# A fused cross-attention and mixture-of-experts kernel: the first batch loaded as fp32 through hardware DMA queues, GpSimd given subtractions, and a new written-out instruction order

## Chip, cores, metric

The kernel runs on one core of a Trainium2 chip. The metric is device time in microseconds, median of several executions. A core has five engines with a queue each, which run their instructions in order: TensorE (PE, with weight loads shown as PEld), VectorE (DVE), ScalarE (ACT), GpSimd (POOL) and SyncE (SP). SP and ACT issue DMAs through hardware queues, POOL through a software queue, which can also convert fp32 to fp16 on the way. Engines wait for one another through semaphores.

## What is computed

The reference, cut to its core (B, H, S, D = 8, 8, 512, 64, with 32 state rows for each head; the second part has 4352 rows of 512, 8 experts, hidden size 1024):

```python
scores = scale * x @ state.T                 # per batch and head
a = softmax(scores, -1);  xread = a @ state  # 512 rows
scores2 = scale * state @ x.T
a2 = softmax(scores2, -1); sread = a2 @ x    # 32 rows
x = concat([xread, sread], 2) -> (B*544, 512)
logits = x @ w_gate; P = exp(logits - max)
for _ in range(8):                           # Sinkhorn: rows, then columns
    P /= P.sum(1) + 1e-9; P /= P.sum(0) + 1e-9; P *= N / E
for e in range(E):
    out += P[:, e:e+1] * (relu(x @ w1[e]) @ w2[e])
```

## The kernel before

All matrix products run in fp16 with fp32 sums. The work has two parts.

**Part one, up to about 134 us, is an order written out by hand.** Every step is an `Op` with the engines that it may run on, and with the steps and buffers it waits for. They are numbered as they are made. `PLAN` is a table of steps, such as `56P`: number 56, on PE (V is DVE, A ACT, G POOL, S the SP queue, H nothing on the device). `issue` walks through `PLAN` and emits one step after the other, so the table sets both the engine of a step and its place in that engine's queue. The figures beside the engines, such as `(0.44, 0.62)`, and attributes such as `since` and `goal` were used by whatever drew the table; they have no effect on the device.

The steps of part one, with their lines:

- *State.* `state` is loaded as fp32 by two DMAs (L441, on SP and ACT, four batches each, in rows of 256 bytes), cast into `st_in` twice side by side (`place`), transposed on PE (L492) and copied into `stT`. `stD`, a block-diagonal form, serves the first two score blocks.
- *x.* Each batch of x is loaded in two halves of four heads, fp32 converted to fp16 by POOL's queue (L468). For batches 0 and 1 PE transposes it (L578) and DVE or ACT copies it out as `xT`; for the others a DMA transpose from SP does (L591).
- *Score blocks S0 to S15,* two for each batch. PE computes scores into one pair of PSUM banks (L605); a second form for the first two blocks is L684. The A side (softmax over the state): DVE transposes (`flip`, L628), maximum (L631), subtraction (`subA`, L648), exp on ACT (L656), sum and reciprocal on DVE (L666, L667), product on DVE or POOL (`normA`, L670), transpose back into `aT` (L674, or PE and a copy for the first two). The B side (softmax over the tokens): maximum (L640), exp on ACT (L652), reciprocal (L659), product (`normB`, L662), DMA transpose of `E2` into `ETs` (L742), and PE's read of x (L758).
- *Expert 0.* V = state times w1 (L870, two halves for each batch), hidden layer hps = V times aT (L897), second layer yps (L935).
- *Gate and Sinkhorn* (L788, L814 to L846), w2 sums of expert 1 for the second part (`sums_w`, L965, eight subtractions on DVE), and the first hidden block of expert 1.

**Part two, from about 134 us, is ordinary loops** over experts 1 to 7 and 9 row blocks: `layer1` (L255 on PE, relu L275 on ACT, sums L281 to L284 on DVE), `layer2` (seven half-size products L334 where there would be eight, added into `acc` by L348), `project` (L235) and `load_w`.

PE is in order, so a step that waits holds all that stands behind it in `PLAN`. The same holds for POOL's queue, in which loads of x and weights stand between its products.

Of the kernel before, what the change touches and what calls it, by code (L numbers as in the profile page):

```python
# [16 lines left out]
6G 0S 1S 2V 7H 44V 3A 33V 32A 34A 8G 56P 36P 35V 55H 37V 10H 45V 57A 42P 58V 9G 38P 40P 43A 59P 4S 39A 41V 5V  # L17
46V 62P 50H 51G 61A 71V 63P 60A 52G 64V 11G 72V 73A 80P 65V 12G 435P 401P 66A 81V 13H 79P 14G 82V 436A 88V
437A 404P 83A 67V 402A 137H 403A 89V 96H 97P 100P 84V 406A 68V 90A 98A 15G 85V 69P 86P 53G 405A 99V 87V 70A
103P 101A 102A 91V 409P 16H 92G 413P 104V 407P 410A 411P 105V 111A 438P 120P 414V 408A 419P 421P 106V 415P  # L20
112V 138S 121V 74V 439A 412A 422V 113V 417P 107A 54G 440A 75G 122V 432P 429P 123V 370V 420A 469P 128A 418A
416A 17G 108V 140P 124A 125V 423P 426P 471A 433P 114A 148V 93S 129V 430P 149V 172H 424P 76S 434A 115V 470A
109G 130V 139S 110V 126G 141V 131A 427P 18G 127V 142V 428V 431A 445P 143V 132V 94P 150A 95V 77P 425A 156P 116G
447P 151V 133V 78V 449P 446A 443P 441P 144A 455P 164V 152G 448A 117S 19H 450V 157V 444A 165V 173S 442A 451P
456A 166A 134S 20G 452A 453P 463P 158V 472P 207H 145V 175P 159V 183V 184V 457P 31G 146G 454A 176V 473A 160A
464P 185A 174S 460P 458P 461P 465A 147V 161V 21G 153S 177V 191P 47P 162G 474A 118P 167V 459A 154P 462A 178V
163V 135P 49A 168G 199V 22H 48V 179A 466P 136A 352P 475P 200V 192V 201A 193V 119V 467P 476A 194V 23G 195A 485P
202V 208S 210P 180V 169S 155A 218V 356P 353A 481P 357V 468A 487P 219V 24G 489P 181G 186V 211V 242H 486A 482A
477P 490V 488A 483P 479P 220A 170P 478A 503P 187G 480A 484V 171A 203G 196V 537P 209S 25H 212V 226P 197G 504A
505A 506P 213V 500P 182V 198V 26G 234V 221V 507A 222V 204S 188S 491P 27G 538A 227V 539A 501P 497P 502A 508A  # L30
492P 235V 243S 228V 244S 214A 229V 511P 215V 236A 523P 230A 498P 494P 216G 245P 495P 515P 512V 499A 277H 231V
524A 493A 517P 246V 253V 223S 496A 247V 521P 516A 237V 254V 519P 509P 522V 518A 248V 513P 232G 189P 520A 255A
205P 510V 224P 514V 540P 28H 278S 261P 249A 190V 269V 29G 225A 270V 262V 531P 534P 206V 238G 250V 532P 256V
358P 271A 535P 217V 541A 533A 233V 542A 312H 279S 263V 272V 536A 354P 280P 528P 543P 529P 525P 288V 289V 251G
555P 264V 281V 265A 282V 239S 257V 526P 359A 266V 544A 530V 556A 545P 355A 547P 549P 273G 553P 527A 546V 571P
313S 290A 548A 283V 605P 550A 554V 296P 267G 606V 304V 572A 305V 240P 573A 557P 284A 607A 558A 551P 297V 552A
568P 360P 258S 241V 285V 30G 291V 306A 559P 562P 574P 298V 252V 315P 299V 286V 569P 576A 268V 323V 563P 575A
274S 300A 560P 570A 292G 316V 361A 561A 581P 564A 307V 565P 362P 324V 317V 301V 325A 302G 566P 363V 582A 326V
579P 587P 583P 287V 314S 588V 591P 567A 580A 639P 608P 584A 592A 347H 303V 331P 577P 348G 641V 640A 610A 609A
339V 293S 589P 585P 275P 332V 259P 578A 327G 586A 260A 590A 294P 340V 308G 333V 341A 593P 309S 318V 319A 334V  # L40
295V 364P 594P 276V 328S 625P 619P 342V 595A 335A 365A 599P 320V 602P 343V 336V 600P 337V 603P 626A 321G 322V
329P 310P 350G 344S 601A 349G 311A 620V 345P 338V 346V 604V 366P 596P 330A 368P 369V 351G 597P 367A 371V 611P
372P 598A 695H 615P 617P 373V 612V 374P 375V 613P 614V 616A 623P 618A 621P 696H 711H 376A 705P 377V 642P 624A
622A 706A 707A 630P 643V 697V 708P 644A 378P 379V 631P 710A 627P 698V 380V 647P 632A 709A 636P 628P 381P 633P
699V 648V 637P 382V 634P 657P 629A 638A 383V 700V 653P 658A 655P 384P 651P 635A 701V 654A 725P 385V 723P 386V
702V 656A 726A 716P 652A 724A 717A 645P 659P 649P 714P 646A 650A 660A 387P 721P 715A 712P 727P 687P 722A 388V
728A 688A 667P 713A 664P 389V 390P 703V 665P 668P 391V 673P 674A 392V 661P 670P 669A 729V 393P 671P 394V 666A
662P 672A 677P 395V 718P 663A 678A 679P 675P 683P 719A 681P 720V 680A 676A 685P 396P 684A 682A 397V 686A 692P
704V 689P 693P 690P 730P 398V 694A 399P 733P 731V 691A 732A 735A 734A 400V
# [55 lines left out]
def issue(ops):  # L105
    for step in PLAN:
        op = ops[int(step[:-1])]
        assert all(d.end for d in op.after) and ENGINES[step[-1]] in op.on
        for slot in op.takes:
            slot.ring.taken.append(slot)  # L110
            slot.tile = slot.make()
        op.emit(ENGINES[step[-1]])
        op.end = True
    assert all(op.end for op in ops) and len(PLAN) == len(ops)
# [3 lines left out]
def kernel(  # L118
# [99 lines left out]
    etp = actx.enter_context(tc.tile_pool(name="attn_et", bufs=3))  # L218
# [216 lines left out]
    st_in = spl.tile([128, B, NQ, 2, D], FP16, name="st_in")  # L435
    st_st = spl.tile([128, B, NQ, D], FP32, name="st_st")
    loads = []
    for g in range(2):
        def load(g=g):
            bs = ds(g * B // 2, B // 2)  # L440
# [3 lines left out]
        loads.append(dma((0, 0), 1.0, load, lands=2.7))  # L444
        ops[-1].since, ops[-1].hard = 0.5, 1
# [5 lines left out]
    wgd = dma((0, 2), 0.1, lambda: nc.sync.dma_start(  # L451
        out=wg_st, in_=moe_w_gate.rearrange("(kc p) e -> p kc e", p=128)))
    wgc = op((15.0,), {"DVE": (0.15, 0.25)}, lambda _: nc.vector.tensor_copy(out=wgh, in_=wg_st), [wgd])
    wgc.since = 20.0
# [7 lines left out]
    for b in range(B):  # L462
        x_ready.append([])
        part("x%d" % b)
        got = op((0, 1 + 2 * b), {"HOST": (0.0, 0.0)}, lambda _: None, takes=[xn[b]])
        for g in range(2):
            def load(b=b, g=g):
# [4 lines left out]
            x_ready[b].append(dma((0, 1 + 2 * b, g), 1.28 if b else 2.3 - 0.6 * g, load, [got], [], [xn[b]], "POOL"))  # L472
            ops[-1].since, ops[-1].hard = 0.7, 1
# [4 lines left out]
    bd = []  # L478
    for g in range(2):
        for s_ in range(2):  # L480
            def place(eng, g=g, s_=s_):
                bs = ds(g * B // 2, B // 2)
                copy(eng, st_in[:, bs, :, s_, :], st_st[:, bs])

            bd.append(op((0, 0, g), {"DVE": (0.50, 0.64)} if s_ else {"ACT": (0.50, 0.65)}, place, loads[g:g + 1] + warmed))
    stT_ready = []
    for g in range(4):
        ps = psum([128, 4, 128], FP16, "stT_ps")

        def turn(_, g=g, ps=ps):  # L490
            for i in range(4):
                nc.tensor.transpose(ps.tile[:, i], st_in[:, 2 * g + i // 2, i % 2].rearrange("p s d -> p (s d)"),  # L492
                                    identh)

        def keep(eng, g=g, ps=ps):
            copy(eng, stT[:, ds(2 * g, 2)].rearrange("p b q c -> p (b q) c"), ps.tile)

        t = op((0, 1, g), {"PE": (0.35, 0.55)}, turn, bd[g // 2 * 2:g // 2 * 2 + 2] + [makeh], [ps])
        stT_ready.append(op((0, 1, g), EVICT16, keep, [t], uses=[ps]))
    ND = (TOK + 1) // 2  # L500
    stD_ready = {}
    if TOK:
        stD = spl.tile([128, ND, NQ, 4, 2, Ns], FP16, name="stD")
        zd = op((0, 0, 0), {"POOL": (0.40, 0.50), "DVE": (0.25, 0.35)}, lambda eng: engines[eng].memset(stD, 0.0))
        for b in range(ND):
            def spread(eng, s_, b=b):
# [4 lines left out]
                               lambda eng, s_=s_, spread=spread: spread(eng, s_), stT_ready[b // 2:b // 2 + 1] + [zd])  # L511
# [55 lines left out]
    for b in range(B):  # L567
# [4 lines left out]
                  [x_ready[b][0]], [xT])  # L572
        for g in range(2 if b < NT else 0):
# [11 lines left out]
            t = op((due_x(2 * b + g) - 2.0, 0), {"PE": (0.70, 0.88)}, turnX, [x_ready[b][g], makeh], [ps], [xn[b]])  # L585
# [3 lines left out]
        for g in range(0 if b < NT else 2):  # L589
# [5 lines left out]
            xt_ready.append([dma((due_x(2 * b - 2), 0, g), 2.0, turn, [x_ready[b][g], gotT], [], [xn[b], xT], lands=0.8)])  # L595
            ops[-1].moves, ops[-1].xbar = (3.0, 0.8), 1
            ops[-1].on = {"SPQ": (1.4, 4.5)}
        for q in range(NQ):
# [18 lines left out]
            o2 = op((due_x(2 * b + q), 0), {"PE": (0.13, 0.38)}, score, xt_ready[q] + stT_ready,  # L617
# [5 lines left out]
            E2 = slot(etp, 3, [128, S], FP16, "E2")  # L623
            a16 = slot(asb, 2, [128, S // 32, Ns], FP16, "a16")
            ETs = slot(etp, 3, [128, NSC, 128], FP16, "ETs")
# [402 lines left out]
    n = 0  # L1028
# [79 lines left out]
```

## Time and profile before

| | |
|---|---|
| median of 3 runs | 754.13 us (753.98 to 754.52) |
| the profiled execution | 753.05 us, of which the profile's span is 751.3 us |
| mean granted TensorE clock | 0.997 |
| PE / DVE / ACT / POOL busy | 98% / 82% / 69% / 9% |
| DMA | 36.71 MB in 51,323 packets |
| first PE instruction | 6.98 us |
| first hidden-layer matmul of expert 0 (L897) | 18.66 us |
| first layer-2 matmul of expert 1 (L334) | 134.45 us |

Busy time is a union of an engine's instructions; PE's are pipelined, so what counts for PE is also how far apart its matmuls start (0.216 us for 128x512 at full clock). Instructions on DVE and ACT overlap a little too: 128x512 in fp32 lasts 0.68 us on DVE, and the next one starts 0.60 us after it. A wait is put down to what released it last. The granted clock is the share of full speed that PE was allowed.

### The profile page before, as it was taken

Reading aid. Unit: us, or ns where it says so; the run is one execution under the profiler, and the core shown is the slowest. Engines: PE = TensorE matmul, PEld = TensorE weight load, DVE = VectorE, ACT = ScalarE, POOL = GpSimd, SP = SyncE. Lnnn points to the kernel's source line nnn. Section 1 sums busy time; section 2 is a strip of 40 time slices with the busy share of each in tenths; the row PEclk is TensorE's granted clock in tenths of the full one; section 3 lists DMA queues with packets and bytes.
Section 4 is the critical chain, followed back from the end, with each engine's and each line's share of the span. In section 5 each row is a group of like instructions: output and inputs, shape, how many; then the busy total and the mean of one; then the engine's idle time right before and its main releaser. Section 6 shows DMA issues by size and latency. Waiting matters only on the chain.

```text
span 751.3 us, 16144 instructions
## 1 busy us (share of the span) xinstructions
PE 734.7 (98%) x6517; PEld 501.2 (67%) x6517; DVE 616.3 (82%) x1529; ACT 518.2 (69%) x1014; POOL 70.8 (9%) x81
## 2 busy tenths in 40 slices
PE   4999999999999999999999999999999999999997
PEld 3444445667677777777777677776777777776776
DVE  5999989888888789788887888887897888878875
ACT  6876846798976766666666766667667666676662
POOL 3664310200010000100000000100001000000000
PEclk9999999999999999999999999999999999999999
DMA  9997560600032000600006000330006000002234
GB/s 175 151 133 127 86 92 1 113 2 1 1 66 48 2 1 2 113 1 1 2 4 110 2 1 1 58 56 1 1 2 112 2 1 2 1 29 101 98 113 141
DMA packets 51323, 36.71 MB, mean 49 GB/s; under 512 B 25392, under 2 KB 43824, under 8 KB 51248
## 3 DMA queue, kind: packets, MB, share of 16 engines
q0 software_dynamic: 22272, 20.97, 18.4%
q1 hardware_dynamic: 27744, 14.18, 7.7%
q8 instruction: 51, 0.84, 0.5%
q10 hardware_dynamic: 1232, 0.52, 0.3%
q14 instruction: 24, 0.20, 0.1%
HBM read 42.48 MB, written 8.91 MB: 68 GB/s over the span
## 4 chain that ended last, share of the span: by engine, by line
PE 91%; DVE 3%; DMA 2%; ACT 1%; POOL 1%; issue 0%; SPq 0%; POOLq 0%; ACTq 0%
PE hps L255 28%; PE Bseed L334 20%; PE A L334 14%; PE E L334 13%; PE yps L935 6%; PE v_ps L235 4%; PE hps L897 4%; DMA xT<-x_nat 2%; DMA x_nat<-in_x_dram 1%; DVE acc L348 1%; ACT Hm L275 1%; PE su_ps L758 0%; PE y L312 0%; PE v_ps L870 0%; POOL E L662 0%; ACT V L419 0%
## 5 line engine op out<-in xcount | busy, mean ns | idle before, releaser
L275 ACT ACTIVATE Hm<-hps 128x512 f16<-128x512 f32 (+1 forms) x496 | 265.2, 577 | 128.1 <-PE hps L255 125.3
L255 PE MATMUL hps<-aT,V 128*128 128x512 f16 x880 | 230.1, 379 | 0.0
L334 PEld LDWEIGHTS <-Hm 128*128 128x128 f16 x1888 | 181.4, 98 | 71.2 <-issue 15.8
L348 DVE SCALAR_TENSOR_TENSOR acc<-Bseed,Pmat,acc 128x256 f32<-128x256 f32 x354 | 155.0, 477 | 9.4 <-PE Bseed L334 6.6
L334 PEld LDWEIGHTS <-sm 128*128 128x128 f16 x1416 | 138.2, 98 | 34.1 <-issue 0.4
L334 PE MATMUL A<-w2h,Hm 128*128 128x256 f16 x944 | 123.7, 273 | 0.0
L334 PE MATMUL Bseed<-T,Hm 128*128 128x256 f16 x944 | 123.3, 273 | 0.0
L255 PEld LDWEIGHTS <-V 128*128 128x128 f16 x880 | 86.1, 98 | 51.3
L348 DVE SCALAR_TENSOR_TENSOR acc<-E,Pmat,acc 128x256 f32<-128x256 f32 x236 | 103.1, 476 | 12.5 <-PE E L334 12.5
L281 DVE TENSOR_TENSOR sm<-Hm 128x512 f16<-128x512 f16 (+1 forms) x122 | 50.1, 411 | 64.2 <-ACT Hm L275 64.0
L243 ACT CAST V<-v_ps 128x512 f16<-128x512 f32 x150 | 77.7, 611 | 0.0
L348 DVE SCALAR_TENSOR_TENSOR acc<-A,Pmat,acc 128x256 f32<-128x256 f32 x118 | 51.9, 479 | 17.2 <-PE A L334 16.7
L935 PE MATMUL yps<-w2h,hT 128*128 128x512 f16 x272 | 64.1, 379 | 0.0
L363 ACT COPY Bseed<-A 128x512 f32<-128x512 f32 (+1 forms) x62 | 34.1, 550 | 43.3 <-PE A L334 42.1
L334 PE MATMUL E<-T,sm 128*128 128x256 f16 x472 | 61.7, 273 | 0.0
L334 PE MATMUL E<-w2h,sm 128*128 128x256 f16 x472 | 61.7, 273 | 0.0
L334 PE MATMUL Bseed<-T,sm 128*128 128x256 f16 x472 | 61.5, 272 | 0.0
L282 DVE TENSOR_TENSOR Hm<-Hm 128x512 f16<-128x512 f16 (+1 forms) x122 | 50.2, 412 | 4.2
L284 DVE TENSOR_TENSOR sm<-Hm,sm 128x512 f16<-128x512 f16 (+1 forms) x122 | 50.2, 412 | 4.2
L283 DVE TENSOR_TENSOR sm<-sm,Hm 128x512 f16<-128x512 f16 (+1 forms) x122 | 49.4, 405 | 0.0
L194 POOL DMA_DIRECT2D w1h<-in_moe_w_dram x12 | 8.5, 714 | 397.9 <-PE hps L255 397.4
L935 PEld LDWEIGHTS <-hT 128*128 128x128 f16 x272 | 25.4, 99 | 28.8 <-issue 1.7
(127 smaller groups left out, 609.7 us busy)
## 6 DMA issues: line engine op xcount, KB each, us to landing
w1h<-in_moe_w_dram POOLq DMA_DIRECT2D x16, 512.0 KB, 7.0
w2h<-in_moe_w_dram POOLq DMA_DIRECT2D x16, 512.0 KB, 8.1
out_dram<-acc SPq DMA_DIRECT2D x32, 256.0 KB, 2.6
x_nat<-in_x_dram POOLq DMA_DIRECT2D x16, 256.0 KB, 5.6
st_st<-in_state_dram ACTq DMA_DIRECT2D x1, 256.0 KB, 4.9
st_st<-in_state_dram SPq DMA_DIRECT2D x1, 256.0 KB, 4.3
ETs<-E SPq DMA_TRANSPOSE x16, 3.9
out_dram<-acc SPq DMA_DIRECT2D x4, 64.0 KB, 1.7
```

Of the source, the lines that this page charges most:

```text
L235: nc.tensor.matmul(ps[q][ds(j * Ns, Ns), :], stT[ds(r, 64), bi, q, ds((j ^ q) * Ns, Ns)], w1h[ds(r, 64), 2 * q + j // 2, cols], tile_posit ...
L243: nc.scalar.copy(out=dst, in_=src)
L255: nc.tensor.matmul(out, lhs, rhs, start=(k == 0), stop=(k == len(terms) - 1))
L275: nc.scalar.activation(out=Hm[:, i, j, :tn], in_=hps[:, :tn], func=AF.Relu)
L281: nc.vector.tensor_add(s1, a21, a22)
L282: nc.vector.tensor_sub(a21, a11, a21)
L283: nc.vector.tensor_sub(s2, s1, a11)
L284: nc.vector.tensor_sub(s4, a12, s2)
L334: nc.tensor.matmul(dst[:, c], lhs(j, c), rhs[:, j], start=first and c == 0 and j == 0, stop=(j == NJ - 1), skip_group_check=True)
L348: nc.vector.scalar_tensor_tensor(out=dst, in0=src[:, c], scalar=p[:, k], in1=dst, op0=ALU.mult, op1=ALU.add)
L363: nc.scalar.copy(out=Bb[:, :nk], in_=A[:, :nk])
L935: nc.tensor.matmul(yps.tile, hT[fb].tile[:, ds(tk * 128, 128)], w2h[:, fb, :], start=(fb == 0), stop=(fb == NFB - 1))
```

## The change

- `PLAN` is another table: nearly all of part one stands in another order. The instructions of part two are the same.
- Batch 0 of x is loaded as raw fp32 by four DMAs of two heads each, two on SP and two on ACT, into rows of `acc` that are not in use yet, and cast to fp16 by DVE and ACT (`narrow`). Batches 1 to 7 go through POOL's queue as before.
- State is laid out in rows of 1 KB and in four groups of two batches. Group 0 is loaded ahead of x0 on SP; group 1 follows behind x0 on SP, groups 2 and 3 go first through POOL's queue. The steps of a batch wait for its own group (`st_ready(b)`), not for all.
- `IDLE` puts 79 dummy matmuls or transposes of the identity in front of eight PE steps of the opening. They write a PSUM tile that the step then overwrites.
- Of 14 `subA`, 11 run on POOL (none before); of the 8 `sums_w`, 5 do. `normB` on POOL is a product of two tensors where it was one with a scalar per row (11 on POOL, 12 before); `normA` has 13 on POOL, 12 before. The memset of `stD` moves to POOL.
- Both copies of `aT` for batch 0 run on DVE (one was on ACT). `E2` and `ETs` have four buffers each, three before. w_gate is loaded once the first state group is in place.
- PE's queue holds 13,166 instructions (13,008 before); the 158 more are the dummies, two each.

```diff
+IDLE = {38: 33, 63: 12, 69: 2, 87: 5, 442: 9, 107: 12, 93: 4, 44: 2}
+XH = 2
+NE2 = 4
...
-    etp = actx.enter_context(tc.tile_pool(name="attn_et", bufs=3))
+    etp = actx.enter_context(tc.tile_pool(name="attn_et", bufs=NE2))
...
-            (nc.scalar if g else nc.sync).dma_start(
-                out=st_st[:, bs], in_=state[bs].rearrange("b (q h) n d -> (h n) b q d", q=NQ))
+    st_rows = state.rearrange("b h (k l) d -> (b h k) (l d)", l=4).rearrange("(g p) c -> p g c", p=128)
+    xs = acc[:, ds(0, 2 * XH), :].rearrange("p (g t) d -> p g (t d)", t=2)
+    def load_st(a, b):
+        return begin("SPQ", lambda: nc.sync.dma_start(out=st_st[:, a:b], in_=st_rows[:, a:b]), 0.35 * (b - a))
+    def load_x(g, k):
+        q = nc.scalar if k else nc.sync
+        return begin("ACT" if k else "SPQ", lambda: q.dma_start(
+            out=xs[:, g, ds(k * 512, 512)].rearrange("p (h c) -> p h c", h=2),
+            in_=x[0, ds(4 * g + 2 * k, 2)].rearrange("h (p sc) d -> p h (sc d)", sc=NSC)), 0.68)
+    loads = load_st(0, 1)
+    xs_in = [[load_x(g, k) for k in range(2)] for g in range(XH)]
+    for a, b in ((1, 2), (2, B // 2)):
+        def load_rest(eng, a=a, b=b):
+            (nc.gpsimd if eng == "POOL" else nc.sync).dma_start(out=st_st[:, a:b], in_=st_rows[:, a:b])
...
+            if not b and g < XH:
+                def narrow(eng, g=g, k=0):
+                    copy(eng, xn[0].tile[:, ds(4 * g + 2 * k, 2), :].rearrange("p h c -> p (h c)"),
+                         xs[:, g, ds(k * 512, 512)])
...
-        t = op((0, 1, g), {"PE": (0.35, 0.55)}, turn, bd[g // 2 * 2:g // 2 * 2 + 2] + [makeh], [ps])
+        t = op((0, 0, g), {"DVE": (0.55, 0.64), "ACT": (0.62, 0.72)}, place, [loads[g]] + warmed)
+        t = op((0, 1, g), {"PE": (0.35, 0.55)}, turn, [t, makeh], [ps])
+    st_ready = lambda b: [stT_ready[b // 2]]
+    wgd = dma((0, 2), 0.1, lambda: nc.sync.dma_start(
+        out=wg_st, in_=moe_w_gate.rearrange("(kc p) e -> p kc e", p=128)), [stT_ready[0]])
...
             def normB(eng, E2=E2, rrec=rrec):
-                engines[eng].tensor_scalar(out=E2.tile, in0=E2.tile, scalar1=rrec.tile, scalar2=None,
-                                           op0=ALU.mult)
+                if eng == "POOL":
+                    nc.gpsimd.tensor_mul(E2.tile, E2.tile, rrec.tile.broadcast_to((128, S)))
+                else:
+                    nc.vector.tensor_scalar(out=E2.tile, in0=E2.tile, scalar1=rrec.tile, scalar2=None, op0=ALU.mult)
...
-                s1 = op(r(4), {"DVE": (0.60, 0.80)}, subA, [m1], [], [eA, mxA])
+                s1 = op(r(4), {"DVE": (0.60, 0.80), "POOL": (1.05, 1.20)}, subA, [m1], [], [eA, mxA])
...
-        nc.vector.tensor_sub(T[:, i, jj], p[:, jj], q[:, jj])
+        engines[eng].tensor_sub(T[:, i, jj], p[:, jj], q[:, jj])
...
+    def idle(t, n):
+        if not n:
+            return
+        t = t.rearrange({2: "p a -> p a", 3: "p a b -> p (a b)", 4: "p a b c -> p (a b c)"}[len(t.shape)])
+        for _ in range(n):
+            if t.dtype == FP16:
+                nc.tensor.transpose(t[:, :128], identh, identh)
+            else:
+                w = min(128, t.shape[1])
+                nc.tensor.matmul(t[:, :w], identh, identh[:, :w], start=True, stop=True, skip_group_check=True)
```

In `IDLE` step 38 is the transpose of the first state group, 63 the transpose of x0's first half, 69 score block S0, 87 the second form of scores for S1, 442 the first half of V for batch 1, 107 the transpose of x1's second half, 93 the transpose of a16 for S1, 44 the transpose of the last state group.

The opening of the new table, as far as the first hidden-layer matmuls on PE and the copies that they wait for:

```python
10H 4A 2A 9G 7V 0S 8A 37A 1S 12A 57H 38P 377V 11V 51G 14A 62H 3S 63P 39A 6G 5S 13V 66P 15H 65V 64V 16G 103H
53A 18H 69P 52A 46A 58G 70P 40V 78V 47P 79V 67A 68A 43A 17G 80A 87P 48A 71V 59G 41P 104P 42A 88V 86P 72V 442P
```

More of the change, by code (lines that the diff above doesn't have):

```diff
@@ L111, in issue @@
             slot.tile = slot.make()
+        idle(op.takes[0].tile if op.takes else None, IDLE.get(int(step[:-1]), 0))
         op.emit(ENGINES[step[-1]])
@@ L432, in dma, with begin @@
         return o
[L435 to L440, printed above, removed]
-            (nc.scalar if g else nc.sync).dma_start(
-                out=st_st[:, bs], in_=state[bs].rearrange("b (q h) n d -> (h n) b q d", q=NQ))
-        loads.append(dma((0, 0), 1.0, load, lands=2.7))
-        ops[-1].since, ops[-1].hard = 0.5, 1
+    st_in = spl.tile([128, B // 2, 4, 2, D], FP16, name="st_in")
+    st_st = spl.tile([128, B // 2, 4 * D], FP32, name="st_st")
+    st_rows = state.rearrange("b h (k l) d -> (b h k) (l d)", l=4).rearrange("(g p) c -> p g c", p=128)
+    xs = acc[:, ds(0, 2 * XH), :].rearrange("p (g t) d -> p g (t d)", t=2)
+    def begin(queue, emit, us):
+        o = dma((0, 0), us, emit, lands=0.7)
+        o.on = {queue: (0.48, 3.0)}
+        o.since, o.hard = 0.72, 1
+        return [o]
+    def load_st(a, b):
[10 more added lines that the diff above has]
+            (nc.gpsimd if eng == "POOL" else nc.sync).dma_start(out=st_st[:, a:b], in_=st_rows[:, a:b])
+        o = op((1, a), {"POOL": (0.78, 4.0), "SPQ": (0.48, 3.0)}, load_rest)
+        o.moves, o.since, o.hard = (0.35 * (b - a), 1.2), 0.72, 1
+        loads += [o] * (b - a)
     warm = spl.tile([128, 1], FP32, name="warm")
@@ L466 @@
         for g in range(2):
+            if not b and g < XH:
+                def narrow(eng, g=g, k=0):
+                    copy(eng, xn[0].tile[:, ds(4 * g + 2 * k, 2), :].rearrange("p h c -> p (h c)"),
+                         xs[:, g, ds(k * 512, 512)])
+                x_ready[0] += [[op((0, 1, g), {"DVE": (0.50, 0.60), "ACT": (0.62, 0.72)},
+                                   lambda eng, k=k, narrow=narrow: narrow(eng, k=k), xs_in[g][k] + warmed + [got], [], [xn[0]])
+                                for k in range(2)]]
+                continue
             def load(b=b, g=g):
@@ L811 @@
     part("ones")
-    op((30.0,), {"DVE": (0.2, 0.3)}, lambda _: nc.vector.memset(ones128, 1.0))
+    ones = op((30.0,), {"DVE": (0.1, 0.25)}, lambda _: nc.vector.memset(ones128, 1.0))
     part("K")
@@ L970 @@
     tdone = op((due_1, 1), {"HOST": (0.0, 0.0)}, make_t, [room] + w2_ready(1))
-    for i in range(4):
-        for g in range(2):
-            tdone = op((due_1, 1), {"DVE": (0.40, 0.50)}, lambda _, i=i, g=g: sums_w(i, g), [tdone])
-    tdone.goal = -0.9
+    for g in range(2):
+        tg = []
+        for i in range(4):
+            tg.append(op((due_1, 1), {"DVE": (0.42, 0.52), "POOL": (1.06, 1.20)}, lambda eng, i=i, g=g: sums_w(eng, i, g),
+                         [tdone] + tg[i - 1:i] * (i == 1) + tg[1:2] * (i == 3)))
+            tg[-1].goal = -0.9
     for bi in range(2):
```

132 lines of the change are left out of this document (62 added, 70 removed).

## The prediction

> **What bounds the kernel now.** I read the page first, then busy time by stretches, then PE's waits, then the timeline of the opening.
>
> ```profile
> span 751.3 us, 16144 instructions
> PE 734.7 (98%) x6517; PEld 501.2 (67%) x6517; DVE 616.3 (82%) x1529; ACT 518.2 (69%) x1014; POOL 70.8 (9%) x81
> ```
>
> PE is idle for 16.6 us of the span. Only time in which PE stands, or runs at a lower clock, can be won.
>
> The stretches are cut at the first PE instruction (6.98), at three clock changes (10.03, 16.83, 20.24), at the first hidden-layer matmul L897 (18.66) and at the first layer-2 matmul of expert 1, L334 (134.45). Columns: start and end, length, busy time of PE, weight loads, DVE, ACT, POOL, then granted clock, DMA, GB/s.
>
> ```profile
> 0.00:6.98 6.98, 0.00 (x0) 0.00 (x1) 1.47 (x4) 2.64 (x4) 6.23 (x14) 1.00 0.88 137
> 6.98:10.03 3.05, 3.05 (x29) 3.05 (x30) 1.25 (x4) 1.66 (x3) 1.28 (x2) 1.00 1.25 193
> 10.03:16.83 6.80, 4.22 (x78) 2.31 (x75) 6.50 (x16) 5.66 (x12) 0.00 (x0) 1.00 1.36 198
> 16.83:20.24 3.41, 3.14 (x21) 1.47 (x21) 2.96 (x7) 3.28 (x9) 1.28 (x1) 0.50 1.34 204
> 18.66:134.45 115.79, 113.28 (x1099) 54.32 (x1099) 105.20 (x252) 83.86 (x184) 43.90 (x41) 0.99 0.65 96
> 134.45:747.30 612.85, 612.62 (x5306) 440.61 (x5298) 499.85 (x1252) 422.58 (x808) 19.35 (x25) 1.00 0.17 36
> ```
>
> From 134.45 PE never waits and the change leaves that code alone: 751.3 - 134.45 = 616.85 us stay. From 18.66 to 134.45 PE stands 2.5 us in all. Ahead of 18.66 it does nothing for 6.98 us, and in 10.03:16.83 it is 62% busy while DVE is 96% busy: there DVE is what everything waits for. In 16.83:20.24 the clock is halved, and the first hidden matmuls fall into it.
>
> PE's waits before 134.45, by releaser (total, times, longest):
>
> ```profile
> PE xT_ps L578 <- DMA x_nat<-in_x_dram: 8.1, 3, 7.0
> PE psB L605 <- DMA xT<-x_nat: 2.2, 3, 0.9
> PE psB L605 <- ACT E L652: 0.6, 1, 0.6
> ```
>
> The opening in the timeline (start, length):
>
> ```profile
> 6.98 1.04 PE L578 MATMUL xT_ps<-identh,x_nat 128*128 128x128 f16 x8 [6.98 <-DMA x_nat<-in_x_dram]
> ...
> 9.41 0.78 PEld L578 LDWEIGHTS <-x_nat 128*128 128x128 f16 x8
> ...
> 10.29 0.30 PE L605 MATMUL psB<-xT,stT 64*32 64x256 f16 x8
> ...
> 10.67 0.69 DVE L640 TENSOR_REDUCE nmB<-psB 128x1 f32<-128x512 f32 x1 [0.16 <-PE psB L605]
> ...
> 14.84 0.45 PEld L578 LDWEIGHTS <-x_nat 128*128 128x128 f16 x8 [0.67 <-DMA x_nat<-in_x_dram]
> ...
> 18.28 0.42 DVE L421 COPY aT<-aT_ps 128x512 f16<-128x512 f16 x1 [0.19 <-PE aT_ps L709]
> ...
> 18.66 2.65 PE L897 MATMUL hps<-aT,V 128*128 128x512 f16 x8
> ...
> 21.69 1.90 PE L897 MATMUL hps<-aT,V 128*128 128x512 f16 x8
> ...
> 26.16 1.04 POOL L670 TENSOR_TENSOR a<-eA,rA 128x512 f16<-128x512 f32 x1 [0.70 <-DVE rA L667]
> ```
>
> So: x0 lands at 6.98, first scores at 10.29, DVE works without a pause from 10.67 to 18.70, and the aT copy releases the first hidden matmul. From there PE is full. The same eight matmuls take 2.65 us at the low clock and 1.90 later: 0.75 us lost.
>
> **Term A, when the first hidden matmul starts.** The state of two batches (128 KB in 1 KB rows) and x0 (1 MB fp32) now go through SP and ACT. In before, hardware packets begin at 1.95 and the state lands 0.7 us behind its last packet. Rate bounds: the halves of x1 land 1.37 us apart, 0.5 MB of source each, so 380 KB/us; the state's 0.5 MB in 256-byte rows takes 1.95 to 4.6, so 190 KB/us. The x0 loads are 1 KB pieces as x is in before, so I take the fast end. 1.15 MB then end at 1.95 + 3.0 = 5.0, landing at 5.7; at the slow end 8.0 and 8.7. The heads that the first transposes need come next to last: 5.4, or 7.5.
>
> Then a cast L419/L421 (0.62), 8 transposes (0.45 at full clock plus 0.3 until a reader starts; 0.85 plus 0.3 cold) and two xT copies on DVE (0.34 apart, 0.42 the last). From 5.4 this gives scores at 5.4 + 0.62 + 0.75 + 0.76 = 7.5. But PE first has 33 dummies from 1.4 (identh is done at 1.29): at the cold spacing of 0.107 (L492: 1.71 for 16) until 4.9, four state transposes to 5.35, twelve more dummies to 6.65, or 6.0 if warm. Transposes at 6.65 cold: 7.8, scores at 8.6. Between 7.5 and 8.6, slow end 9.7; I take 8.2, against 10.29: the start itself wins 2.1 us.
>
> DVE then gives most of this back. From the scores to the last aT copy it does all it did in before (8.37 us from 10.29 to 18.66) and, by the new order, one more STREAM_TRANSPOSE L628 (0.63 start to start, for the third score block), one more xT copy and the aT copy that ACT did (0.34 each), and it casts a piece of state (0.6) just ahead of the first maximum, of which I let 0.3 show: 8.37 + 1.31 + 0.3 = 10.0. First hidden matmul at 8.2 + 10.0 = 18.2 instead of 18.66: **-0.45** (17.5 to 19.7: -1.2 to +1.0).
>
> **Term B, work done by then.** PE has by then also done the fourth score block and one more V half, 0.23 and 0.22 us in the timeline's spacing. From there it is full as before: **-0.45**.
>
> **Term C, the clock.** 79 dummies stand in front of the steps named in IDLE: 33 + 12 ahead of the first transposes, 34 at 0.056 us = 1.9 us in the gaps up to V1. They hide in the 2.6 us that PE stands in 10.03:16.83; without that cover they cost these 1.9 us. If they hold the clock, the 0.75 us at 18.66 are won; if it falls again, 0. I take **-0.7**: between 10 and 18 PE now has the dummies, the fourth scores and a further V half.
>
> The Trainium skill, TensorE: Matmul & The Clock Gate, Part 4 (PE-mode transpose), says that a transpose does not count as PE activity and leaves the clock low, and 63 of the 79 dummies are transposes. The trace disagrees: 6.98:10.03 holds transposes alone, and the weight loads go from 0.78 us for eight (9.41) to 0.45 (14.84), with the rise at 10.0 (the clock column has no record before that and shows 1.00). By that page A and C would come out as in the second rival.
>
> **Term D, waits from 18.66 to 134.45.** GpSimd takes 11 of 14 subtractions L648 and 5 of 8 w2 sums L965: 11 x 0.60 + 5 x 0.34 = 8.3 us off DVE, but DVE is not what PE waits for there. On GpSimd each is priced by L670, 1.05 us; below it stands nothing, above it L662 with 1.56. normB turns from L662's form into L670's: 11 x 0.5 = 5.5 us less. In all GpSimd's compute goes from 32 to about 42 us of 116: room, but its queue also issues x, and each attention step gets 0.4 us longer. The sums have cover: GpSimd has nothing to do from 100 to 134, and their reader, E of L334, starts at 136.27. PE's 2.2 us of waiting on transposed x stay as likely as before. With the Sinkhorn chain starting earlier I take **-0.3** (-2.2, all waits gone, to +2.5, as many again).
>
> Hidden edits at 0: the other state (128 KB on SP behind x0, 256 KB first on POOL) lands by 7 and is needed at 8 to 10; w1 lands at 10.5 and 14.5 instead of 10.89 and 13.43 while its second half is used at 17, behind DVE; SP's w_gate load waits for the first stT copy (7) and only the x2 transpose stands behind it, whose data come at 16; a fourth E2/ETs buffer, finer waits on state, and the ones memset cost nothing. The memset of stD delays POOL's first DMA by 0.4 us, in front of x1, needed at 11.
>
> Sum: -0.45 - 0.45 - 0.7 - 0.3 = **-1.9**. The profiled execution took 753.05 (its span and 1.75 around it), so 751.15; it lies 1.08 below the median 754.13, which makes **752.2**. About 0.2% (1.5 us) is what a measurement of this kernel tells from no change.
>
> **Rivals.**
> 1. Late x0: the slow DMA end. A +1.0, B, and C -0.45 for a half-warm clock: 754.1 - 0.2 = 754.0, no change. For: 16 DMA engines are busy from 2.5 us on in either kernel, and the x1 and w1 loads now compete with x0. Against: 1 KB rows. Chance 0.18.
> 2. Dummy transposes do not warm PE. Scores at 8.6 or later and twice 0.4 more for T0 and T1, so A is +0.4; C is 0; B and D stay: 754.1 - 0.35 = 753.8. Chance 0.07, as 6.98:10.03 speaks against it.
> 3. Slower: GpSimd holds up x. A load of x stands on POOL behind a subtraction that waits for DVE; its transpose comes late, and PE stands in order at the score block. In before 3 of the 12 score blocks S4 to S15 wait, 2.2 us, 0.73 each. If nine wait: +4.4 on top, less 1.6 won in the opening: 756.9. It decides from seven waits of twelve; slower by over 0.2% from eight. For: the attention is packed tighter and POOL's chain is three instructions a step. Against: the x loads of before wait for buffers, not for POOL. Chance 0.17.
> 4. More: scores at 7.5 with no state cast in the way (A -1.2) and none of the waits on xT left (D -2.2): 749.6. Chance 0.10.
>
> **The numbers.** The forecast has 0.48. Its terms reach from 751.2 to 753.8 as A and D move, so some 0.41 of it is faster by over 0.2%. Faster 0.41 + 0.10 + 0.02 (rival 1 with an early clock) = 0.53; slower 0.17 + 0.01 = 0.18; same the rest, 0.29. The range goes from 749.7 to 755.6: it leaves out the half of rival 4 and most of rival 3.
>
> **What would show it.** After: first scores near 8.2, first L897-like matmul near 18.2 and eight of them in 1.9 us; clock 1.00 in 10 to 20; first L334 near 132.5; about 617 us behind it; no xT wait above 0.9 us. Wrong if the scores come at 10 or later, if the clock record shows 0.50 between 10 and 20, or if score blocks wait for xT more than four times.

## The result: 756.26 us, 0.3% slower

The changed kernel takes 756.26 us (median of 15 runs, 753.84 to 759.06), the kernel before beside it 753.98 (752.16 to 756.05). The ratio is 1.0033, 95% interval 1.002 to 1.0047. The forecast was 752.2 with a range to 755.6, so both its sign and its range were wrong. The profiled execution took 758.11 us, 5.06 more than that of before and 1.85 above its own median. The sums below are made between the two profiled executions; in the medians the loss is less than half as large. The four executions of the changed kernel with a mean granted clock of 0.999 or more are its four fastest (753.84 to 754.90); the other eleven took 755.09 to 759.06.

Lines have moved: scores L605 is now L635, hidden layer L897 is L929, second layer yps L935 is L967, V L870 is L902, the x transposes on PE L578 are L608 and by DMA L591 are L621, layer 2 of part two L334 is L338, `project` L235 is L239.

The head of the page:

```profile
span 756.3 us, 16307 instructions
PE 740.9 (98%) x6596; PEld 507.3 (67%) x6596; DVE 614.6 (81%) x1520; ACT 514.8 (68%) x1010; POOL 80.2 (11%) x97
```

Busy time by stretches, cut at the first scores (8.97), the first hidden-layer matmul (18.61), the score block S4 (22.19 to 25.60 is the gap ahead of it), the clock changes (27.05, 30.47) and the first layer-2 matmul (138.54). Columns as before: start and end, length, PE, weight loads, DVE, ACT, POOL, granted clock, DMA share, GB/s.

```profile
0.00:8.97 8.97, 6.49 (x67) 6.22 (x67) 2.04 (x7) 5.05 (x10) 6.43 (x14) 1.00 0.86 217
8.97:18.61 9.64, 7.80 (x151) 5.39 (x149) 9.41 (x22) 9.54 (x21) 1.39 (x2) 1.00 1.30 202
18.61:22.19 3.58, 3.58 (x24) 1.51 (x25) 3.29 (x8) 3.58 (x8) 2.23 (x3) 1.00 0.82 90
22.19:25.60 3.41, 0.38 (x9) 0.09 (x9) 1.41 (x5) 2.97 (x7) 2.80 (x3) 1.00 1.30 197
27.05:30.47 3.42, 3.42 (x10) 1.22 (x8) 3.35 (x13) 1.42 (x4) 2.73 (x3) 0.50 1.18 185
18.61:138.54 119.93, 113.94 (x1083) 55.09 (x1083) 102.45 (x239) 77.35 (x174) 53.07 (x57) 0.99 0.66 92
138.54:752.30 613.76, 612.62 (x5306) 440.54 (x5298) 500.36 (x1255) 422.87 (x809) 19.34 (x25) 1.00 0.17 36
```

PE's waits up to 142 us, by releaser (total, times, longest; three rows of the view, no other has more than 1.3 us):

```profile
PE psB L635 <- DMA xT<-x_nat: 4.4, 2, 3.0
PE xT_ps L608 <- DVE x_nat L425: 1.1, 1, 1.1
PE v_ps L239 <- DVE V L425: 0.7, 1, 0.7
```

And the timeline of PE at the three places that matter:

```profile
18.61 3.63 PE L929 MATMUL hps<-aT,V 128*128 128x512 f16 x16
22.16 0.41 PE L902 MATMUL v_ps<-w1h,stT 64*32 64x512 f16 x8
25.60 0.30 PE L635 MATMUL psB<-xT,stT 64*32 64x256 f16 x8 [3.03 <-DMA xT<-x_nat]
26.47 4.88 PE L967 MATMUL yps<-w2h,hT 128*128 128x512 f16 x14
...
69.35 0.30 PE L635 MATMUL psB<-xT,stT 64*32 64x256 f16 x8 [1.41 <-DMA xT<-x_nat]
...
140.54 0.62 PE L239 MATMUL v_ps<-w1h,stT 64*32 64x512 f16 x16 [0.73 <-DVE V L425]
```

The opening does what it was expected to do: scores 1.3 us earlier, sixteen hidden matmuls at full clock in 3.63 us where before eight took 2.65. Then PE reaches S4 at 22.2 and stands 3.0 us for the DMA transpose of x2, the clock is at half for 3.42 us from 27.05, 1.45 us after PE has started again, PE stands once more at S12, and layer 2 starts at 138.54 instead of 134.45. Behind it a further 0.9 us (0.73 of it shown as a wait) go at the seam to part two, where the first V of `project` waits for a V copy on DVE.

### The profile page after: what moved, and what is told of

It is laid out like the page before. It is cut to its first block, busy times and chain, and to the rows that moved or that the text cites. A ratio compares the mean times of both kernels' runs of the same rounds, so it can differ in the third digit from the quotient of the medians.

```text
span 756.3 us, 16307 instructions
## 1 busy us (share of the span) xinstructions
PE 740.9 (98%) x6596; PEld 507.3 (67%) x6596; DVE 614.6 (81%) x1520; ACT 514.8 (68%) x1010; POOL 80.2 (11%) x97
## 4 chain that ended last, share of the span: by engine, by line
PE 86%; DVE 7%; DMA 4%; ACT 1%; POOL 1%; issue 0%; SPq 0%; POOLq 0%; ACTq 0%
PE hps L259 27%; PE Bseed L338 20%; PE A L338 14%; PE E L338 13%; PE yps L967 4%; PE v_ps L239 4%; PE hps L929 2%; DMA xT<-x_nat 2%; DMA x_nat<-in_x_dram 2%; ACT Hm L279 1%; DVE acc L352 1%; DVE hT L431 1%; DVE nmB L670 0%; DVE aT L706 0%; PE y L316 0%
## 5 line engine op out<-in xcount | busy, mean ns | idle before, releaser
L338 PEld LDWEIGHTS <-Hm 128*128 128x128 f16 x1888 | 181.3, 98 | 71.3 <-issue 16.0
L352 DVE SCALAR_TENSOR_TENSOR acc<-Bseed,Pmat,acc 128x256 f32<-128x256 f32 x354 | 154.9, 477 | 10.4 <-PE Bseed L338 6.7
L338 PEld LDWEIGHTS <-sm 128*128 128x128 f16 x1416 | 138.2, 98 | 34.1 <-issue 0.4
L338 PE MATMUL A<-w2h,Hm 128*128 128x256 f16 x944 | 123.7, 273 | 0.0
L338 PE MATMUL Bseed<-T,Hm 128*128 128x256 f16 x944 | 123.3, 273 | 0.0
L967 PE MATMUL yps<-w2h,hT 128*128 128x512 f16 x272 | 65.6, 387 | 0.1
L367 ACT COPY Bseed<-A 128x512 f32<-128x512 f32 (+1 forms) x62 | 34.1, 550 | 43.3 <-PE A L338 42.1
L338 PE MATMUL E<-w2h,sm 128*128 128x256 f16 x472 | 61.7, 273 | 0.0
L338 PE MATMUL E<-T,sm 128*128 128x256 f16 x472 | 61.7, 273 | 0.0
L338 PE MATMUL Bseed<-T,sm 128*128 128x256 f16 x472 | 61.5, 272 | 0.0
L967 PEld LDWEIGHTS <-hT 128*128 128x128 f16 x272 | 26.2, 100 | 30.0 <-issue 2.9
```

The costliest lines, as they stand in the source:

```text
L338: nc.tensor.matmul(dst[:, c], lhs(j, c), rhs[:, j], start=first and c == 0 and j == 0, stop=(j == NJ - 1), skip_group_check=True)
L352: nc.vector.scalar_tensor_tensor(out=dst, in0=src[:, c], scalar=p[:, k], in1=dst, op0=ALU.mult, op1=ALU.add)
L367: nc.scalar.copy(out=Bb[:, :nk], in_=A[:, :nk])
L967: nc.tensor.matmul(yps.tile, hT[fb].tile[:, ds(tk * 128, 128)], w2h[:, fb, :], start=(fb == 0), stop=(fb == NFB - 1))
```

## Experiments

All start from the changed kernel ("after") unless said otherwise. Edits are of `PLAN`; a line of a diff shows only the steps around the edit. Theories: **W**, PE stands in order at single blocks (S4, S12, the seam) and what it stands is lost once and for all; **P**, GpSimd's products hold up the loads of x that stand behind them; **D**, the new opening itself (hardware queues, dummies) costs it; later **Q**, the DMA transpose of x2 is what is late, not x2; **R**, the pace of all loads sets the time and every wait comes back for another transfer. Each result is a median with its ratio to the runs of before on the same chip and the 95% interval; runs on different chips are compared by these ratios. A wait is the profile's idle time in brackets; the expectations count the waits at S12 and at the seam in after from start to start, less the usual distance of two matmuls, and so have 1.74 and 0.89 where the brackets have 1.41 and 0.73.

### S4 later in PE's queue

```diff
-... 476P 425A 82G 50V 147P 415A ... 436P 433P 440P ...
+... 476P 425A 82G 50V 415A ... 436P 433P 147P 155V 156V 148V 440P ...
```

> The changed kernel with score block S4 (step 147 and its three readers on DVE) moved behind the first four quarter-blocks of yps in the order table; nothing else. Theory W (PE stands in order at S4 for the DMA transpose of x2, 3.0 us, and the 3.4 us of half clock that follow cost 1.7 more): PE no longer waits there, no half clock between 7 and 140 us, first L338 near 134 instead of 138.5, time some 3 to 4 us below the changed kernel, 0.998 to 1.000 of the kernel before. Theory P (GpSimd's products hold up the loads of x, and every transpose with them): the wait turns up at the next score blocks, time as the changed kernel, 1.003. Theory D (the opening or its dummies cost it): 1.003.

755.32 us, ratio 1.0018 (1.0004 to 1.0032). In its profile S4 does not wait, there is no half clock in the whole opening, and layer 2 starts at 136.14 instead of 138.54. But yps now waits 1.1 us for w2 up to 28.18 and S5 1.2 us for its transpose up to 32.16; S12 (1.6 us) and the seam (0.7 us) stay. W holds for part of the loss; the rest turned into waits for later transfers.

### Subtractions back on DVE

```diff
-... 113G ... 130G ... 150G ... 341G ...
+... 113V ... 130V ... 150V ... 341V ...
```

> The changed kernel with all 14 subtractions L678 on DVE, none on GpSimd. Theory P: the xT waits of PE fall by more than half and the time by 2 us or more, to 1.000. Theory W: S4 still waits 3 us, since x2 has left GpSimd's queue at 6 us and the transposes are late for another reason; time as the changed kernel or up to 2 us more, for DVE has 11 times 0.6 us more: 1.003 to 1.006.

760.95 us, ratio 1.0085 (1.0066 to 1.0104). S4 still waits 2.5 us. In this order the subtractions on GpSimd are worth about 4 us (3.9 by the ratios); they are not the cost. The loss is also larger than W had it.

### No dummies

```diff
-IDLE = {38: 33, 63: 12, 69: 2, 87: 5, 442: 9, 107: 12, 93: 4, 44: 2}
+IDLE = {}
```

> The changed kernel without its 79 dummies. Theory W with the clock as predicted: the first rise of the clock comes at 9 to 12 us instead of 6.6, first scores 0 to 0.5 us earlier or later, the clock falls to half once between 13 and 20, first hidden matmuls at half clock, S4 still waits but shorter by what is lost ahead of it; time 0 to 1 us above the changed kernel, 1.003 to 1.005. Theory D (the dummies cost time in the opening): 1 to 2 us less, 1.000 to 1.002.

756.13 us, ratio 1.0037 (1.0023 to 1.0051), as after: in this order the dummies make no difference that can be measured, though without them the first full clock in the records comes at 11.4 us instead of 6.6. In this run's profile the transpose of x2 took only 4.4 us and S4 did not wait; PE stood 3.0 us up to 39.40 instead, at the read of x for an ETs transpose, with half clock from 38.7 to 45.6. The place of the long wait is not fixed, but it is again a DMA transpose.

### First half of x2 ahead of w1's second half

```diff
-... 59G ... 19G ...
+... 19G 59G ...
```

> The changed kernel with the load of x2's first half ahead of the second half of w1 in GpSimd's queue; nothing else. Theory W: x2 lands near 15.8 instead of 18.3 and its DMA transpose is issued then and lands near 22 to 23, so S4 waits under 0.5 us; the second half of w1 lands near 18.3 instead of 17.0 and costs 1.3 us at V in the opening; no half clock after S4; in all 2 to 4 us less than the changed kernel, 0.998 to 1.001. Theory P and D: 1.003 or 1 us worse.

754.88 us, ratio 1.0015 (1.0004 to 1.0026). x2's transpose is issued at 14.98 and lands at 21.22, S4 does not wait. V now waits 1.5 us for w1, up to 17.51, and the clock is halved from 17.06 to 20.47. S12 (1.2 us) and the seam (0.7 us) stay.

### Second half of x2 ahead of GpSimd's product

```diff
-... 99G ... 20G ...
+... 20G 99G ...
```

> The second half of x2 is issued ahead of the GpSimd product of B1, behind which it stood for 11 us. Theory P (GpSimd's products hold the x loads): it lands near 20 instead of 23.88, its transpose near 26 instead of 29.97, the wait at S4 falls under 1.5 us and the time to about 755. Theory W (PE stands in order at S4 for the transpose of the first half, which this edit doesn't touch): S4 still waits 2.5 to 3.5 us, the time stays within 1 us of 756.3.

759.23 us, ratio 1.0072 (1.0053 to 1.0091). P in this form falls, and the run goes the other way: the load that no longer stands behind the product lands 1.9 us earlier, but the transpose of the *first* half now takes 9.7 us instead of 7.3, and S4 waits 4.2 us. That GpSimd's product kept a load back did x2 good.

### Seam copy on ACT, x6's transpose earlier on SP

```diff
-... 284H ... 230S ... 285S ... 741V ...
+... 284H 285S 230S ... 741A ...
```

> Two waits late in the attention are taken away: the last V copy goes to ACT (0.89 us of PE standing at the first V L239), and the transpose of x6's first half is put ahead of the step of SP that waits for GpSimd's product of B8 (1.74 us at S12). Theory W (each PE wait is lost once and for all): both waits gone, first L338 about 1.7 earlier than after for the same S4 wait, 753.9. Rival (the waits are slack that the next stage takes back): the waits move to another block, the time stays at 755.5 to 756.5.

754.60 us, ratio 1.0009 (0.9996 to 1.0022). The wait at S12 is gone. The one at the seam is not: the first V of `project` waits 0.8 us for the same copy, now on ACT behind two others. S4 still waits 1.4 us, and a wait of 2.3 us has turned up at 39.33, for an ETs transpose, with half clock from 39.65 to 43.06. The time lies between W's 753.9 and the rival's 755.5: W holds for S12, the rival in part. SP's waits and SP's timeline in after, from 50 to 66 us, show what held x6's transpose:

```profile
SPq L774 <- POOL E L693: 5.4, 1, 5.4
```

```profile
62.14 1.19 SPq L774 DMA_TRANSPOSE ETs<-E  x1
63.42 1.27 SPq L621 DMA_TRANSPOSE xT<-x_nat  x1
```

The ETs transpose stood 5.4 us for the product, and x6's transpose (63.42) went out right behind it. So a product on GpSimd did hold up a transpose of x, through SP and not through POOL's loads.

### All of these together

```diff
-... 59G ... 19G 60G ... 99G ... 20G ... 61G ... 230S ... 285S ... 741V
+... 19G 59G 60G ... 20G 61G 99G ... 285S 230S ... 741A
```

> x2's first half ahead of w1's second half, its second half and w2's second half ahead of the product of B1, and both edits of the other kernel (last V copy on ACT, x6's transpose earlier on SP). Theory W and P together: no wait at S4 and S12 and none at the seam; 754.9 of the first-half edit alone less 0.9 and 1.5 is 752.5, faster than before. Rival (waits come back elsewhere, at V or yps for w): 754 to 755.

757.69 us, ratio 1.0049 (1.0031 to 1.0067). The forecast of W and P together fails. It does not test W by itself, for S4 was not freed: the transpose of x2 is issued at 15.06, but with four software loads still under way it lands at 26.75, 11.7 us later, and S4 waits 2.6 us. V waits 1.3 us for w1 besides, and the seam still 0.8.

### x0 through GpSimd's queue as before

```diff
-XH = 2
+XH = 0
-10H 4A 2A 9G 7V 0S 8A 37A 1S 12A ... 51G 14A ... 3S ... 13V
+6H 5G 3V 0S 4A 31A ... 7G 8G 45G ...
```

(With four loads and four casts fewer, two software loads 7G and 8G, and the other steps renumbered.)

> x0 goes through GpSimd's queue with the cast on the way, as in before; all else as in after. Theory D (the hardware queues spoil the opening: x0 and the state share the engines with x1, w1, x2): no loss, 755 to 756.3. Theory W with P: the loads behind it on GpSimd come 1.5 us later, S0 near 10.4 and S4 waits 4 us or more: 757.5 to 758.5.

759.06 us, ratio 1.0089 (1.0057 to 1.0121). D falls: without the hardware queues the time is no lower. What they are worth stays open. The kernel is 2.8 us behind after in the medians and 4.2 by the ratios, but its six runs spread from 757.59 to 764.76, and the opening in its profile is no later than in after: scores at 8.06, first hidden matmul at 18.52, x2's first half landed at 18.20. The expectation's "S0 near 10.4" was not met. The transpose of x2 takes 8.0 us there; S4 waits 3.8 us and S12 1.3.

### x2 transposed by PE

```diff
-NT_ = 2
+NT_ = 3
-... 145S ... 428P ... 439P ... 146S ...
+... 145P 146V 147A 432P ... 148P 149V 150A 443P ...
```

(Steps from 147 on are renumbered by 4.)

> x2 is transposed on TensorE (two times eight transposes and four copies) instead of by two DMA transposes; the rest is as in after. Theory Q (PE stands at S4 for the DMA transpose, which took 7.3 us beside the loads of x2 and w2, not for x2 itself, which landed at 18.3): no wait at S4 over 0.5 us, no half clock behind it; 3.0 and 1.7 us won, 0.9 us of transposes and up to 1 us of copies on DVE paid: 753.5 to 754.5. Rival R (everything that is loaded in the opening comes at the rate of the DMA engines, and PE now waits for w2 or x3 instead): 755.5 or more.

754.45 us, ratio 1.0012 (1.0000 to 1.0024): Q. x2's data are there in time; S4 does not wait and the clock stays full. S12 still waits 1.1 us, the seam 0.8.

### w2's first half behind x2's second

```diff
-... 19G ... 60G 99G ... 20G ... 61G
+... 19G ... 99G ... 20G 60G ... 61G
```

> w2's first half is issued behind x2's second half, so behind GpSimd's product of B1: when the transpose of x2's first half is issued (18.3) one load less is ahead of it. Theory Q: the transpose takes 5 us instead of 7.3, S4 waits 1 us instead of 3, x2's second half lands 2 us earlier; but yps of B0 may wait for w2 by about 1 us: 755. Rival (the transpose's time does not hang on the loads beside it): S4 waits 3 us as in after and w2's wait comes on top, 757.

759.92 us, ratio 1.0082 (1.0063 to 1.01). The opposite of what Q gave: three software loads are now issued at 17.5 to 19.0, just as the transpose is, and it takes 8.4 us. What counts is what moves beside it, not how many loads are issued ahead.

### x2 first, S12 and the seam mended

```diff
-... 59G ... 19G ... 230S ... 285S ... 721P 722A 700P 697P ... 737P 739A 740P 407V 741V 738A 742A
+... 19G 59G ... 285S 230S ... 737P 739A 740P 741V 738A 742A 721P 722A 700P 697P ...
```

> x2's first half issued ahead of w1's second half (754.9 when alone), x6's transpose ahead of the SP step that waits for the product of B8 (1.5 us at S12), and the last V matmuls with their copies ahead of the last eight yps matmuls (0.89 us at the first V L239). Each wait is lost once and for all (theory W): 752.5. Rival (slack that a later stage takes back): 754 to 755.

753.71 us, ratio 1.0003 (0.9991 to 1.0015). The three waits are gone and some 1 us is won against the run of x2 first alone, less than half of the 2.4 expected. The time lies between W's 752.5 and the rival's 754 to 755. The 1.5 us for w1 ahead of the hidden layer stay.

### The subtractions alone, in the kernel before

```diff
-... 106V ... 123V ... 143V ... 334V
+... 106G ... 123G ... 143G ... 334G
```

> The kernel before with one part of the change alone: the subtractions of A2 to A4, A6 to A8, A10 to A12, A14 and A15 go to GpSimd, at the same places of the order. If GpSimd's subtractions hold up the loads of x (theory P): slower, 755 or more, with waits at score blocks. If DVE is what PE waits for in the attention: faster, 752 to 753.5. If neither: 754.

758.84 us, ratio 1.0069 (1.0052 to 1.0086). Without an order made for it the same part costs 5 us: a score block at 42.1 waits 3.2 us behind an exponential on ACT, the one at 66 2.6 us for a transpose. P's forecast, slower with waits at score blocks, came true here. What holds the blocks is an exponential and a transpose; SP, which issues the transposes, has itself stood 5.5 us for a product on GpSimd (L742 for L670).

```profile
PE psB L605 <- ACT eA L656: 3.2, 1, 3.2
PE psB L605 <- DMA xT<-x_nat: 2.6, 1, 2.6
```

### x2 on PE, S12 and the seam mended

The edits of the two kernels "x2 transposed by PE" and "x2 first", without the move of 19G.

> x2 transposed on TensorE (754.45 when alone), x6's DMA transpose ahead of the SP step that waits for the product of B8 (1.46 us stand at S12 in the run of x2 alone), the last V matmuls and copies ahead of the last eight yps matmuls (0.91 us at the first V L239 there). Theory W (what PE stands is lost once and for all, and these waits are what the change lost): 754.45 - 1.46 - 0.91 = 752.1, below the kernel before. Rival R (the loads' rate sets the pace and the waits come back for another transfer): 753.5 to 754.5.

**751.92 us** (751.47 to 753.73), ratio **0.9984** (0.9975 to 0.9993): faster than both kernels, 0.2 from the 752.1 of W, and R falls. Its page, then its PE at S4 (L636) and at the seam (L240):

```profile
span 750.7 us, 16337 instructions
PE 739.6 (99%) x6612; PEld 506.6 (67%) x6612; DVE 616.2 (82%) x1522; ACT 515.8 (69%) x1012; POOL 80.3 (11%) x97
```

```profile
18.96 2.76 PE L930 MATMUL hps<-aT,V 128*128 128x512 f16 x12
21.56 0.61 PE L609 MATMUL xT_ps<-identh,x_nat 128*128 128x128 f16 x8
...
23.19 0.40 PE L636 MATMUL psB<-xT,stT 64*32 64x256 f16 x8
...
133.68 1.03 PE L339 MATMUL A<-w2h,Hm 128*128 128x256 f16 x8
...
134.86 0.63 PE L240 MATMUL v_ps<-w1h,stT 64*32 64x512 f16 x16
```

No bracket stands behind S4 or behind the first V of `project`: neither waits. Layer 2 starts at 133.68, 0.77 earlier than before.

### The w2 sums on DVE

```diff
-... 704G ... 709G 707G ... 706G 711G ...
+... 704V ... 709V 707V ... 706V 711V ...
```

> As after, but the five sums of w2 that the change gave to GpSimd are on DVE. If they are cover work as the prediction had it: 756.3 give or take 1. If DVE is late at the seam (the last V copy stands on DVE behind the sums and the column step of Sinkhorn, 0.89 us of waiting): 0.4 to 1.7 us slower, 757 to 758, with a longer wait at the first V L239. If GpSimd is late with the sums: faster.

756.96 us, ratio 1.0047 (1.0031 to 1.0063). The interval overlaps that of after: no effect shown either way, and the seam waits 0.75 us as in after. That the sums on DVE lengthen this wait is not borne out; whether they cost nothing is not decided.

### The fastest kernel without the dummies

> The first kernel of this call without the dummies. If they are worth their place when no wait follows (term C, 0.75 us, plus the faster start): 752.9 to 753.3 against its 752.1, with a half clock at the first hidden matmuls. If they are worth nothing, as in the run without them in the order of after: the same within 0.4 us.

753.35 us, ratio 1.0000 (0.9991 to 1.0009), 1.43 more than with them. Stretches of the kernel with dummies, then of the one without (the figure behind POOL's is the clock):

```profile
14.00:18.00 4.00, 2.28 (x42) 1.66 (x42) 3.73 (x10) 3.38 (x9) 0.95 (x1) 1.00 1.31 203
18.00:22.00 4.00, 3.91 (x40) 1.88 (x38) 3.21 (x6) 4.00 (x9) 2.63 (x4) 1.00 0.89 129
```

```profile
14.00:18.00 4.00, 2.92 (x42) 1.70 (x41) 3.76 (x10) 3.68 (x10) 1.10 (x2) 0.55 1.31 205
18.00:22.00 4.00, 4.00 (x26) 1.39 (x17) 2.53 (x5) 3.28 (x8) 2.48 (x3) 0.60 0.94 130
```

The same dummies that did nothing measurable in the order of after are worth something here: 1.43 us, or 1.2 by the ratios, where term C had 0.7. They hold the clock. With them 10 of 12 executions had a mean granted clock of 0.999 or more, without them 1 of 11. In the order of after they raise it too (4 of 15 with them, none of 12 without), yet the medians there are alike; why the gain is lost in that order was not tried.

## Why the prediction was wrong, step by step

**Term A** (first hidden matmul 18.2, -0.45): measured 18.61, -0.05. The scores came at 8.97, not 8.2: the cast of x0's last piece, which landed only at 7.80 in the trace, held the second eight transposes (the 1.1 us in the waits). The chain from there took 9.64 us, forecast 10.0. This is one profile: in six other runs whose edits leave PE's order up to there alone the first hidden matmul came at 17.7 to 18.6, so 18.2 lies among them. The reading behind the estimate was off as well: the state's packets in before run from 1.87 to 5.00 and not to 4.6, some 170 KB/us, and the packets of x0 and the state in after from 1.77 to 7.64 for 1.31 MB, some 220 KB/us, near the slow end of what was reckoned with.

**Term B** (-0.45): the fourth score block and V half do stand ahead of the hidden layer, at 17.78 and 17.90 in the timeline.

**Term C** (-0.7): the clock was full from 10 to 20 and the sixteen matmuls took 3.63 us, as said. The Trainium skill, TensorE: Matmul & The Clock Gate, Part 4 (PE-mode transpose), would have had the transposes among the dummies leave the clock low; the full clock at 6.57 with them, behind nothing but transposes, speaks against it, as 6.98:10.03 did in before. What the term lacked is the second fall at 27.05, behind the gap of 3.4 us at S4: 3.42 us at half clock, 1.7 lost.

**Term D is the step that failed.** It took -0.3 for 18.66 to the start of layer 2, with +2.5 as its far end, from "PE's 2.2 us of waiting on transposed x stay as likely as before". The stretch grew by 4.14 us in the profiles: PE stands 119.93 - 113.94 = 5.99 us in it instead of 2.51, and is busy 0.66 us more, where 1.71 of half clock instead of 0.79, less term B's 0.45, make 0.47. The mistake was to take a wait as a chance event that keeps its size. The order of after puts S4 directly behind the sixteen hidden matmuls and one V half, at 22.2, and x2 had no reason to be there sooner: the loads of the opening ran at 202 GB/s (198 in before), and x2's first half landed at 18.27, later than the 17.44 of before. The transpose on top took 7.3 us in this profile, 5.8 in before. My hidden edits at 0 said that its data "come at 16"; w1 was said to land at 10.5 and 14.5 and landed at 12.54 and 16.95. What was won ahead of S4 was thus given back at S4. The run with x2 on PE shows that it was the transpose and not the data: that run lost the wait and 1.6 us (by the ratios) with the loads in the same order. That run and the two mended places together came out 3.7 us below after, by the ratios.

**The seam.** "From 134.45 PE never waits and the change leaves that code alone" holds for the code, not for what releases its first instruction. V's last matmuls end by 138.6 in after, but the copy of them that is on DVE stands behind two sums of the hidden block and the column step of Sinkhorn and starts at 139.80 (in before DVE took its copy at 133.92, ahead of that step): 617.76 us behind the start of layer 2 instead of 616.85, 0.9 us. With the 4.1 us of the earlier stretch this is all but 0.1 of the 5.06.

**Rival 3** (GpSimd holds up x, 756.9) had the right number and half of the mechanism. That the number was right is luck: nine waits of 0.73 us were added up, and two were measured, of 3.0 and 1.4 us, with a half clock and the seam beside them. At S12 a product on GpSimd was the holder, but through SP's queue; at S4 it was not, and moving a load past the product made it worse. Rival 1's late x0 showed only in the 0.4 us by which A fell short, rival 2 not at all.

With those waits removed 751.92 was measured, near the forecast of 752.2. That does not confirm the sum: this kernel has three edits more than the change, and term A gave 0.05 of its 0.45 in after's profile. Nor were the same three edits tried in the kernel before, so it is not shown how much of the 751.92 is the change and how much they are; in before's profile neither S4 nor the seam waits.

## What to carry to other kernels

When a change lets an in-order engine run ahead, look up the next instruction that waits for a transfer and ask whether that transfer comes earlier too; if not, the gain ends there, whatever its own terms say. Count the transfer by what will move beside it, and look at the instruction on the far side of each seam as well as at the code behind it. A part that does nothing in one order (the dummies here) can be worth over a microsecond in another, so it is to be tried again once the wait behind it is gone.

## What the runs showed of the hardware

**A DMA transpose has no fixed time.** The same one, x2's first half, took from issue to landing:

| loads around it | us |
|---|---|
| as in after (6 runs) | 4.4, 5.2, 5.9, 6.7, 6.8, 7.3 |
| as in before (2 runs) | 5.3, 5.8 |
| x2's first half ahead of w1's second (2 runs) | 6.2, 6.3 |
| x0 by GpSimd: x2's second half issued 0.5 us before the transpose | 8.0 |
| w2's first half held: three loads issued just as the transpose is | 8.4 |
| x2's second half sooner | 9.7 |
| all together: four loads under way when it is issued | 11.7 |

DMA issues of after and of the run "all together" (the last figure is us from issue to landing):

```profile
xT<-x_nat SPq DMA_TRANSPOSE x1, 7.3
```

```profile
xT<-x_nat SPq DMA_TRANSPOSE x1, 11.7
```

With the same loads it differs by 3 us, and S4 waits 0 to 3 us accordingly. The six times are in the order in which GpSimd issues the load of x2's second half. Where that was 0.08 us before the transpose, it took 7.3 us; where it was 0.05, 0.10, 0.38, 0.73 and 1.03 us after it, 6.8, 6.7, 5.9, 5.2 and 4.4. The first and the last of them, after and the run without dummies:

```profile
18.21 0.81 POOL L496 DMA_DIRECT2D x_nat<-in_x_dram  x1
18.29 1.36 SPq L621 DMA_TRANSPOSE xT<-x_nat  x1
```

```profile
17.27 1.35 SPq L621 DMA_TRANSPOSE xT<-x_nat  x1
18.30 0.81 POOL L496 DMA_DIRECT2D x_nat<-in_x_dram  x1
```

In after the load stands behind GpSimd's product of B1 (17.22 to 18.2), so the end of that product sets the moment. This is an order found in seven profiles, the 8.0 of the table with them; no run held the load back to try it. The waits it makes fit the spread of after, 5.2 us between its fastest and slowest execution; with x2 on PE and the other waits mended it is 2.3. With more loads beside it the transpose lies above that band. The Trainium skill, DMA: Bandwidth & Descriptors, section Queues, rings and completion order, says that each DMA engine takes turns between the queues that have work for it, a packet at a time; that a transpose slows down beside software loads agrees with it, but no run here took all loads away from beside one.

**Half clock came behind gaps, and not by their length alone.** It came in stretches of 3.41 us or twice that. In after the wait of 3.0 us at S4 was followed by 3.42 us at 0.50 that began 1.45 us after PE had started again. Of the eleven PE waits of 2.2 us or more behind 10 us in the kept profiles nine have a half clock beside them, which began between 2.0 us before PE's next start (w2's first half held: 24.07, PE at 26.04) and 1.6 us after it. The two of the kernel before with the subtractions alone, 3.2 and 2.6 us, have none. Shorter waits had it too: with x2 first, 1.4 and 1.5 us, up to 14.88 and 17.51, with half clock from 17.06 to 20.47; with S4 later, 1.5 and 1.6 us had none. What besides the length decides was not tried.
